# A long convolution with a routed expert on one core: placing products, gathers, fused scores, block loads and spectrum stores put elsewhere

## The chip, the cores and the metric

The kernel runs on one core of a Trainium2 chip. Its time is the device time of one execution in microseconds (us); the median of a few executions is given. The core has a matrix engine (TensorE, PE in the profile; PEld is its weight load), a vector engine (VectorE, DVE), a scalar engine (ScalarE, ACT), a general engine (GpSimd, POOL) and a queue engine (SyncE, SP) that here issues nearly all transfers. Each engine works through its own instructions in order, and waits for the others by semaphores. Transfers run on 16 DMA engines.

## The reference

Four sequences x and v of 12608 rows and 128 channels. A filter is made from position features, and applied along each sequence as a causal convolution (by FFT in the reference); the result is multiplied by x. Then a gate scores every row, the 128 best rows of each sequence go through a two-layer network, and its output, weighted by a sigmoid of the score, is added to those rows.

```python
h = (np.maximum(pos_emb @ w1, 0) @ w2) * np.exp(-0.01 * pos)[:, None]
y = irfft(rfft(x * v, 2*S, axis=1) * rfft(h, 2*S, axis=0)[None], 2*S, axis=1)[:, :S]
z = x * y                                      # [4, 12608, 128]
scores = z @ w_gate                            # per batch: the 128 largest, e
out = z;  out[e] += sigmoid(scores[e])[:, None] * (relu(z[e] @ w1m) @ w2m)
```

## The kernel before

**Shape of the work.** The convolution is done as a two-dimensional transform (93 by 125 points) with matrices held in SBUF. The work of one batch is 32 groups of four channels. After its 32 groups a batch has all its transformed outputs in one large SBUF tile, `big` (seen as `ay`, one slice of 2 x 126 x 4 numbers per group), and a column loop finishes it: 16 blocks of eight columns in the order `ORD`, in 32 half blocks h = 0 to 31 of four columns.

**The group step.** The main loop (L1140 to L1230) runs steps t = 0 to 130, over all four batches without a break. Step t holds, in program order: `turn(t - 3)`, the inverse products of the group three steps back (TensorE L515, copied out by ScalarE at L519 into `ay` and at L520 into a small tile); `dft`, the second forward product of group t (TensorE L313; ScalarE copies half of it at L316); hooks for background work; `f_s1(t + 1)`, the first forward product of the next group (TensorE L455, copied by ScalarE at L457); `load_u`, the loads of x and v four groups ahead (SP L292, 250 KB each, x into four buffers and v into two); `f_v`, `f_u` and `f_y`, eight VectorE operations (L464, L461, L471 four times, L473, L475) that combine group t and multiply group t - 1 by the filter's spectrum; on GpSimd `f_sd` (L482, L483, a recombination of group t - 1), `f_c` (L556, corrections of outputs) and `stage_u` (L298, the product x times v of three groups ahead); the loads of spectra (`load_h`, L302, two groups ahead, from the second batch on) and `put`, which moves a quarter of the outputs to other partitions (L532).

**Spectra.** The filter's spectra of the 32 groups are made once at the start, and lie in the upper part of `big` (`hh`, from element 8448 on, 744 elements each). Batch 0 reads them there. They are also stored to a DRAM tile `hd` (L1191, 372 KB each), from which the later batches load them, and batch 0's outputs are then written over them in `big`: group g covers elements 1008 g to 1008 g + 1007, and is written in steps g + 3 and g + 4. Before, step t stores the spectra 4(t-1)//3 up to 4t//3, so that all are stored after step 24.

**The column loop.** After the last group of a batch `P1.run` does for each half block h: `mm` (TensorE L601 and L605), `fin`: a VectorE product with the block of x (L616), and the scores. A score is either weighed and summed, by a product over four columns (L660, on VectorE, or on GpSimd for blocks past column 80) and four ScalarE sums (L670), or, in the last batch for h in `FU`, done by four VectorE products with a sum (L653). When a block is done it is stored to the output by SP (L644, 420 KB), and SP loads the block seven places later into the buffer of the one stored before (L578). Blocks of x for the first places of `ORD` are loaded ahead, during the groups, if their buffer is not one that the groups use: `AHEAD` is (0, 1, 2, 5, 6, 7), in half loads of 210 KB, one in each of the steps that `LA` names (batch 0: 12 in a row; later batches: every second group). The places 3 and 4 use buffers of the group loop and are loaded at the start of the column loop. `comb` (L588) prepares some columns on GpSimd. At h = 29 one `stage_u` is issued.

**Background work.** The top-128 selection of batch b runs during the groups of batch b + 1, as a generator `topk_one` that stops at points marked "e", "d", "n", "t", "p" and "w"; the main loop calls `bg.hook(kind, wait)` at fixed places of a step, and the generator goes on if it stands at that kind and at least `wait` steps have passed. At the end stands `place`: at "p" 16 matmuls (L308) multiply the ranks with a one-hot matrix that VectorE finishes at L944, then at "e" points five small VectorE steps (L954, L958, L964) make the row indices `ix`. At "w" `gather` (L973) lets GpSimd issue an indirect load of the chosen rows into `xe`. The chosen rows of the first three batches are used in the last column loop (h = 4, 8, 12 and 14); the fourth batch's selection stands alone at the end. Before each column loop, and at the first step after the last group (t = 128), `bg.drain` runs what is left.

**Order.** The order of all instructions on each engine is the program's order; semaphores are set where data overlap.

Of the kernel before, what the change touches and what calls it, by code (L numbers as in the profile page):

```python
# [23 lines left out]
NG = 32  # L24
# [14 lines left out]
NU, NV, NX, NH = 4, 2, 5, 3  # L39
# [4 lines left out]
Q4 = 4  # L44
NC, CO = 4, 2
NE = 2
LA = [range(32 - 14, 32 - 2)] + 3 * [range(6, 30, 2)]
NS, ND = 64, 4
SW = 50
NWARM = 8  # L50
# [3 lines left out]
CB = [k for k in ORD[2:] if k < JB]  # L54
NL, NM = 28, 7
DW = (4, 14)
FU = (7, 13, 19, 24, 28)
OFF, _o = {}, 0
for _n, _k, _w in (("te", 2, 2 * HW), ("qs", 2, HW), ("mt", 1, 2 * HW), ("yz", 2, 2 * HW), ("ws", 1, 2 * HW), ("sd", 2, 2 * HW),
                   ("ht", NH, 2 * HW), ("xa", NX, 8 * D), ("wx", 2, HB * D), ("cm", 2, 2 * NC * D), ("x", NU, XC), ("v", NV, XC)):  # L60
# [4 lines left out]
XE = [CE, OFF["yz"][0] + 2 * HW]  # L65
CE = [XE[0] + 8 * D, XE[1] + 8 * D]
XB = [OFF["xa"][0] + k * 8 * D for k in range(NX)] + XE
XB = [OFF["wx"][0]] + [XB[(i + NX - 2) % (NX + 2)] for i in range(len(ORD) - 1)]
AHEAD = [i for i in range(NX + 3) if XB[i] not in XE]
TE0, FS0, XC0 = 0, 4 * KC * FO, 4 * KC * FO + 2 * Q4 * 8 * FO  # L70
POS0, W0, HB0, WM0, CF0 = 0, PJ * NR, 8080, 8080 + N3 * FO, 8080 + N3 * (FO + 1)
HH0 = D * 2 * NJ - NG * 2 * HC
# [144 lines left out]
def hyena_moe(ctx, tc, xg, x2, pos, bw, ww, wg, mw1, mw2, cs, c1, gx, cf, ci, wm, tk, out):  # L217
# [18 lines left out]
    def buf(name, k, shape):  # L236
        o, n, w = OFF[name]
        return view(arena, o + k % n * w, shape)

    def small(shape, name, dt=F32, tag=None):  # L240
        return sp.tile(shape, dt, tag=tag, name=name, bufs=2 if tag == "sc" else 1)
# [8 lines left out]
    def ps2(k, shape, name):  # L250
        return view(bank2[k], 0, shape)

    def gap(n):
        return bank1[1][:, HC:HC + n]
# [39 lines left out]
    def stage_u(t):  # L294
        if t >= B * NG:
            return
        x, v = buf("x", t, [NP, XC]), buf("v", t, [NP, XC])
        nc.gpsimd.tensor_tensor(out=x, in0=x, in1=v, op=ALU.mult)  # L298
# [262 lines left out]
    class P1:  # L561
# [46 lines left out]
        def fin(self, h):  # L608
# [7 lines left out]
            nc.vector.tensor_tensor(out=xa[:, js], in0=self.s4.pop(h)[:, :n], in1=xa[:, js], op=ALU.mult)  # L616
            if self.last and h in FU:
                self.weigh()
# [56 lines left out]
        def run(self, ex):  # L675
            self.last = ex is not None
            self.ring = (0, 1, 2) if ex else (3, 2, 0, 1)
            self.wx = [OFF["wx"][0], OFF["wx"][0] + HB * D, OFF["te"][0] + (2 * HW if ex else 0),
                       OFF["sd"][0] if ex else OFF["ht"][0] + ((self.b + 1) * NG + 2) % NH * 2 * HW]
            self.wg = ps2(2, [128, D], f"wg_{self.b}")  # L680
            nc.scalar.copy(out=self.wg, in_=wgb)
            for i in range(NX + 3):
                if i not in AHEAD:
                    self.load_a(i)
            for k in range(2):
                self.comb()
            for h in range(len(self.hbs)):
                self.mm(h)
                self.fin(h)
                if h == 29:  # L690
                    stage_u((self.b + 1) * NG + 5)
                if ex:
                    ex.hook(h, self.wg)
            self.weigh()
            if ex:
                self.mask()
# [3 lines left out]
    class Background:  # L700
# [7 lines left out]
                self.kind = next(self.gen, None)  # L708
                self.at = self.now

        def drain(self):
            while self.kind is not None:
                self.hook(self.kind)

    def tots(rhs, lhs, n, nm, k):
# [256 lines left out]
    def gather(b, ix, xe):  # L972
        nc.gpsimd.indirect_dma_start(out=xe, out_offset=None, in_=of[:(b + 1) * PR * NJ],  # L973
                                     in_offset=bass.IndirectOffsetOnAxis(ap=ix, axis=0))
# [112 lines left out]
    def topk_one(b, p1, ex):  # L1087
        sc = p1.sc
        for a in range(0, len(p1.late), NM):
            yield "e"  # L1090
            p1.sums(p1.late[a:a + NM])
            yield "n"
        if p1.late:
            yield "d"
            m = gap(NJ)
            nc.scalar.copy(out=m, in_=negm)
            yield "e"
            p1.mask(m)
        f = small([128, NJ], f"f_{b}", tag="f")
        hi, *ms = (small([128, NJ], f"{t}_{b}", BF16, tag=t) for t in ("hi", "ms0", "ms1"))  # L1100
        k = (TopKS if b + 1 < B else TopK)(b, sc, onesb, f, hi, ms)
        k.ex = ex
        if ex:
            ex.start()
        yield from k.rounds()
        yield "n"
        if ex:
            xe = view(arena, OFF["yz"][0], [128, D])
            gather(b, ex.picked[0][1], xe)
        else:  # L1110
            xe = small([128, D], f"xe_{b}", tag=f"xe{b}")
        ws = buf("ws", 0, [128, 640])
        rk, oh = yield from select(b, k, NJ, tri, onesb, rst, ws)
        ix = yield from place(b, rk, oh, jio, NJ, 3, ws[:, :128])
        yield "w"
        gather(b, ix, xe)
        if ex:
            warm(NWARM)
            ex.one(b, ix, xe)
        else:  # L1120
            picked.append((b, ix, xe))
# [5 lines left out]
    bg = Background(iter(()))  # L1127
# [11 lines left out]
    for t in range(NT + LAG):  # L1139
        g = t % NG  # L1140
        i = t - LAG
        bg.now = t
        done = turn(i) if i >= 0 else []
        if t < NT:
            pq = [bank2[2 - 2 * (t % 2) + e] for e in range(2)]
            spare[0] = [a[:, 512 - NS:] for a in bank1]
            uv[t] = [a[:, :HC] for a in pq]
            qs = dft(t, te.pop(t), uv[t])
            if t == 0:
                rest()  # L1150
            bg.hook("p", 1)
            spare[0] = [pq[0][:, HC:]]
            bg.hook("t", 1)
            spare[0] = [a[:, 512 - NS:] for a in bank1]
            bg.hook("n", 1)
            for k in ((1, 2), (3,), (4,), (5,), ())[t] if t < 5 else (t + 1,):
                if k < NT:
                    te[k] = f_s1(k, ps=banks[6:] if k == 2 else bank1)
            spare[0] = None
            bg.hook("w", 1)  # L1160
            if t != 4:
                load_u(t + NU + (t < 4))
            if 0 <= t - 4 < len(fills):
                z = fills[t - 4]
                nc.scalar.activation(out=z, in_=one.to_broadcast([128, z.shape[1]]), func=AF.Copy, scale=0.0)
            o = t - 1 in uv
            if o:
                steps = f_y(t - 1, uv.pop(t - 1))
                y = next(steps)
                next(steps)  # L1170
            small_steps()
            f_v(uv[t], qs)
            if o:
                next(steps)
            bg.hook("e")
            f_u(uv[t], qs)
            seam = i >= 0 and i % NG == NG - 1
            now = [k for k in done if seam or k % NG == NG - 3]
            done_ = [k for k in done if k not in now]
            for k in now:  # L1180
                f_c(k)
            if o or t - 1 in ys:
                sd[t - 1] = f_sd(t - 1, y if o else ys.pop(t - 1))
            for k in done_:
                f_c(k, (ALU.subtract,))
            if not seam and t != 4:
                stage_u(t + 3 + (t < 4))
            for k in done_:
                f_c(k, (ALU.add,))
            for k in range(4 * (t - 1) // 3, min(4 * t // 3, NG)) if t else ():  # L1190
                nc.sync.dma_start(hd[:, k], hh[:, k].rearrange("p e s i -> p (e s i)"))  # L1191
            load_h(t + 2)
            for k in due + [k for k in done if k % NG >= NG - 3]:
                put(k, *((JM, NJ) if k % NG >= NG - 3 else ()))
            due = [k for k in done if k % NG < NG - 3]
            for _ in range(NE):
                bg.hook("e")
            if i >= 0 and i % NG == NG - 1:
                *_, ys[t] = f_y(t, uv.pop(t))
            if t == NT - 1:  # L1200
                sd[t] = f_last(t, uv.pop(t))
        if t >= NT:
            for k in due:
                put(k)
            due = []
            for k in done:
                f_c(k)
                put(k, *((JM, NJ) if k % NG >= NG - 3 else ()))
        if t == NT:
            bg.drain()  # L1210
            ex = Experts(picked)
        if t >= NT:
            for _ in range((3, 1, 0)[t - NT]):
                bg.hook("p")
                bg.hook("t")
                small_steps()
            bg.hook("w", 1)
        b = i // NG
        if i >= 0 and i % NG in LA[b]:
            if i % NG == LA[b][0]:  # L1220
                ph[b] = P1(b)
            k, e = divmod(LA[b].index(i % NG), 2)
            ph[b].load_a(AHEAD[k], e * HB, (e + 1) * HB)
        if i % NG == NG - 1 and i >= 0:
            bg.drain()
            p1 = ph.pop(b)
            p1.run(ex)
            bg = Background(topk_one(b, p1, ex))
    while bg.kind is not None:
        bg.hook(bg.kind)  # L1230
# [49 lines left out]
```

## Time and profile before

| | |
|---|---|
| time, median of 3 (lowest, highest) | 810.06 us (808.38, 812.73) |
| the profiled execution: its time, its span | 810.49 us, 808.6 us |
| granted TensorE clock, mean | 0.993 |
| busy: TensorE, VectorE, GpSimd, ScalarE | 96%, 86%, 76%, 71% |
| filter spectra made and first groups | to about 93 us |
| column loops | from about 231, 398, 568 and 726 us |
| selection of the last batch and its expert | from about 768 us |
| moved by DMA | 189.91 MB, mean 235 GB/s |

The profile is of one execution. Times are from the start of the span. A row of the timeline is one instruction or several equal ones in a row (x48), with its start, its length, engine, line, operation, what it writes and reads, and in brackets how long its engine stood idle before it and who ended that. Lengths of consecutive operations on one engine overlap somewhat, so a pace is read from starts. "issue" as the one waited for means that the profile shows nobody. SPq is a transfer's issue.

### The profile page before, as it was taken

The page shows a single profiled execution, that of the slowest core. Times are in us where ns is not written, and L with a number is a line of the kernel's source. Part 1 is how long each engine was busy: PE and PEld are TensorE (multiplying, and loading weights), DVE is VectorE, ACT ScalarE, POOL GpSimd, SP SyncE. Part 2 cuts the span into 40 slices and gives each one's busy share as a digit, 9 for nine tenths or more (in the row PEclk, how much of TensorE's full clock was granted, in tenths as well). Part 3 has the DMA queues.
Part 4 walks back from the last instruction along what each step waited for, and adds up shares of the span by engine and source line. Part 5 has one row for each costly group of instructions (what it writes and reads, how often), then busy time and mean ns, then how long its engine had stood idle before and what let it go on. Part 6 is the DMA issues. An engine that isn't in the chain of part 4 may idle for free. (4 is left out here: it accounts for less than half of the span.)

```text
span 808.6 us, 41568 instructions
## 1 busy us (share of the span) xinstructions
PE 775.7 (96%) x17154; PEld 651.5 (81%) x17154; DVE 698.7 (86%) x1713; ACT 576.4 (71%) x2269; POOL 618.1 (76%) x694
## 2 busy tenths in 40 slices
PE   8999999999999999999999998999999999989986
PEld 8999767987789678777898786877997787769865
DVE  7454699999879899999898999899999999988973
ACT  0345667665669889975699897866798988747751
POOL 1100189999979799998997998889987999987711
PEclk9999999999999999999999999999999999999998
DMA  9100279999978899998889899898898999847810
GB/s 323 64 27 3 85 238 294 308 307 269 254 240 268 288 263 279 292 293 242 244 274 311 258 286 258 251 280 253 255 301 268 283 287 282 266 124 236 280 48 14
DMA packets 82909, 189.91 MB, mean 235 GB/s; under 512 B 10552, under 2 KB 46264, under 8 KB 82720
## 3 DMA queue, kind: packets, MB, share of 16 engines
q1 hardware_dynamic: 82432, 186.67, 75.2%
q8 instruction: 135, 2.21, 1.2%
q0 software_dynamic: 288, 0.59, 0.3%
q14 instruction: 54, 0.44, 0.2%
HBM read 136.26 MB, written 39.55 MB: 217 GB/s over the span
## 5 line engine op out<-in xcount | busy, mean ns | idle before, releaser
L515 PE MATMUL b<-ci_sb,arena 128*31 128x126 f32 x6080 | 200.4, 271 | 7.8 <-issue 5.6
L455 PE MATMUL a<-c_sb,arena 128*32 128x186 f32 x4064 | 194.7, 321 | 4.0 <-issue 3.4
L298 POOL TENSOR_TENSOR arena<-arena 128x500 f32<-128x500 f32 x128 | 162.4, 1269 | 42.9 <-DMA arena<-in_xg_dram 42.8
L313 PE MATMUL c<-arena,cf_sb 128*32 128x372 f32 x2032 | 194.0, 477 | 0.9 <-DVE arena L473 0.6
L515 PEld LDWEIGHTS b<-ci_sb,arena 128*31 128x31 f32 x6080 | 177.9, 109 | 18.9 <-issue 8.9
L482 POOL TENSOR_TENSOR arena<-arena 128x372 f32<-128x372 f32 x127 | 116.2, 915 | 85.8 <-DVE arena L475 77.6
L457 ACT COPY arena<-a 128x372 f32<-128x372 f32 x252 | 119.9, 476 | 86.6 <-PE a L455 81.5
L455 PEld LDWEIGHTS a<-c_sb,arena 128*32 128x32 f32 x4064 | 139.4, 109 | 46.0 <-issue 20.0
L670 ACT ACTIVATE arena<-arena 128x128 f32<-128x128 f32 x479 | 140.7, 296 | 19.2 <-DVE arena L660 15.7
L519 ACT COPY big<-b 128x412 f32<-128x412 f32 x190 | 108.5, 573 | 19.0 <-PE b L515 17.2
L483 POOL TENSOR_TENSOR arena<-arena 128x372 f32<-128x372 f32 x127 | 115.8, 912 | 0.0
L313 PEld LDWEIGHTS c<-arena,cf_sb 128*32 128x32 f32 x2032 | 78.3, 109 | 44.1 <-issue 17.1
L556 POOL TENSOR_TENSOR big<-big,arena 128x184 f32<-128x184 f32 x192 | 112.5, 587 | 1.2
L471 DVE TENSOR_TENSOR c<-c,arena 128x372 f32<-128x372 f32 x190 | 103.3, 544 | 0.0
L471 DVE TENSOR_TENSOR arena<-c,arena 128x372 f32<-128x372 f32 x190 | 101.5, 534 | 0.0
L464 DVE TENSOR_TENSOR c<-c,arena 128x372 f32<-128x372 f32 x128 | 70.2, 549 | 23.1 <-ACT arena L316 17.7
L670 ACT ACTIVATION_READ_ACCUMULATOR arena<-arena 128x1 f32 x479 | 90.0, 188 | 0.0
L588 POOL TENSOR_TENSOR arena<-big 96x512 f32<-96x512 f32 x64 | 79.5, 1271 | 0.1
L461 DVE TENSOR_TENSOR c<-c,arena 128x372 f32<-128x372 f32 x128 | 70.1, 548 | 0.2
L316 ACT COPY arena<-c 128x372 f32<-128x372 f32 x128 | 61.2, 478 | 12.5 <-PE c L313 10.0
L473 DVE TENSOR_TENSOR arena<-c,arena 128x372 f32<-128x372 f32 x127 | 67.6, 533 | 0.0
L475 DVE TENSOR_TENSOR arena<-arena,c 128x372 f32<-128x372 f32 x127 | 67.4, 530 | 0.0
(216 smaller groups left out, 1262.8 us busy)
## 6 DMA issues: line engine op xcount, KB each, us to landing
arena<-in_xg_dram SPq DMA_DIRECT2D x256, 250.0 KB, 4.7
arena<-hd SPq DMA_DIRECT2D x96, 372.0 KB, 5.1
out_dram<-arena SPq DMA_DIRECT2D x60, 420.0 KB, 5.6
arena<-in_x_dram SPq DMA_DIRECT2D x36, 420.0 KB, 4.9
hd<-big SPq DMA_DIRECT2D x32, 372.0 KB, 5.0
big<-big SPq DMA_DIRECT2D x84, 126.0 KB, 5.2
arena<-in_x_dram SPq DMA_DIRECT2D x48, 210.0 KB, 5.2
big<-in_pos_dram SPq DMA_DIRECT2D x7, 496.0 KB, 7.5
```

The lines of the kernel that those rows point to most:

```text
L298: nc.gpsimd.tensor_tensor(out=x, in0=x, in1=v, op=ALU.mult)
L313: nc.tensor.matmul(pq[w][a:a + 32], lhsT=cf_sb[:, 2 * w + a // NQ, a % NQ:a % NQ + 32], rhs=te[:, a // NQ], start=True, stop=True)
L455: nc.tensor.matmul(tps[s // 2][c, s % 2], lhsT=u[:, s, c], rhs=c1_sb[:, k], start=True, stop=True)
L457: nc.scalar.copy(out=te[:, :, 2 * h:2 * h + 2].rearrange("p e s i -> p s e i"), in_=tps[h])
L471: nc.vector.tensor_tensor(out=o, in0=uv[e], in1=ht[:, k], op=ALU.mult)
L482: eng.tensor_tensor(out=nat(sd[:, 0]), in0=nat(yz[:, 0]), in1=rev(yz[:, 1]), op=ALU.add)
L483: eng.tensor_tensor(out=nat(sd[:, 1]), in0=rev(yz[:, 0]), in1=nat(yz[:, 1]), op=ALU.subtract)
L515: nc.tensor.matmul(o3[32 * k:32 * k + NT3, s % 2, e * NJ:(e + 1) * NJ], lhsT=d[:, e, s, c], rhs=ci_sb[:, e], start=True, stop=True)
L519: nc.scalar.copy(out=ay[:, t % NG, :NJ + JM, ss], in_=o3[:, :, :NJ + JM].rearrange("p s x -> p x s"))
L556: nc.gpsimd.tensor_tensor(out=d if op == ALU.subtract else a, in0=a, in1=stg(t), op=op)
L588: nc.gpsimd.tensor_tensor(out=cm[:KP, e].rearrange("p j (g s) -> p j g s", s=4), in0=av[0], in1=av[1], op=op)
L670: nc.scalar.activation(out=x, in_=x, func=AF.Copy, accum_out=self.sc[:, j:j + 1])
```

## The change

- `LA` and `AHEAD`: four places (0, 1, 2, 5) are loaded ahead in place of six, in eight half loads: in batch 0 in the last eight steps in which it was done before, in the later batches after every third group. Places 6 and 7 are loaded at the start of `P1.run`, behind places 3 and 4.
- `FU`: of the last batch's half blocks 13, 24 and 28 have fused scores; 7 and 19 are weighed and summed.
- The hook for "p" waits for two steps.
- The hook for "w" in the group step is gone. In the column loop one stands after h = 29, behind the `stage_u` there; the drain before the column loop stops at "w", and a full drain stands behind the loop. The third batch's gather is then run by the drain at t = 128.
- The spectra are stored one in each of the steps 1 to 32.

```diff
-LA = [range(32 - 14, 32 - 2)] + 3 * [range(6, 30, 2)]
+LA = [range(32 - 10, 32 - 2)] + 3 * [range(6, 30, 3)]
-FU = (7, 13, 19, 24, 28)
+FU = (13, 24, 28)
-AHEAD = [i for i in range(NX + 3) if XB[i] not in XE]
+AHEAD = [i for i in range(NX + 3) if XB[i] not in XE][:4]
...
                 if h == 29:
                     stage_u((self.b + 1) * NG + 5)
+                    bg.hook("w")
...
-        def drain(self):
-            while self.kind is not None:
+        def drain(self, upto=None):
+            while self.kind not in (None, upto):
                 self.hook(self.kind)
...
-            bg.hook("p", 1)
+            bg.hook("p", 2)
...
             spare[0] = None
-            bg.hook("w", 1)
...
-            for k in range(4 * (t - 1) // 3, min(4 * t // 3, NG)) if t else ():
+            for k in range(t - 1, t) if 0 < t <= NG else ():
                 nc.sync.dma_start(hd[:, k], hh[:, k].rearrange("p e s i -> p (e s i)"))
...
-            bg.drain()
+            bg.drain("w")
             p1 = ph.pop(b)
             p1.run(ex)
+            bg.drain()
```

## Rows read from the trace of the kernel before

**Rows 1.** Stages: stretch, length, each engine's busy us (instructions), clock, DMA share, GB/s.

```profile
189.00:231.00 42.00, 38.82 (x922) 31.08 (x916) 35.01 (x76) 24.20 (x59) 38.37 (x48) 1.00 0.92 249
399.00:410.00 11.00, 11.00 (x207) 11.00 (x204) 10.42 (x18) 9.38 (x63) 10.34 (x10) 1.00 0.78 222
```

**Rows 2.** Timeline, batch 0: inverse products and the first VectorE operation of two steps.

```profile
132.70 0.54 DVE L464 TENSOR_TENSOR c<-c,arena 128x372 f32<-128x372 f32 x1
133.16 1.48 PE L515 MATMUL b<-ci_sb,arena 128*31 128x126 f32 x48
136.31 0.54 DVE L464 TENSOR_TENSOR c<-c,arena 128x372 f32<-128x372 f32 x1
136.97 1.48 PE L515 MATMUL b<-ci_sb,arena 128*31 128x126 f32 x48
```

**Rows 3.** Timeline: the placing products in the second batch's groups, and VectorE beside them.

```profile
370.83 0.54 DVE L471 TENSOR_TENSOR arena<-c,arena 128x372 f32<-128x372 f32 x1
370.98 0.43 PE L308 MATMUL a<-arena 128*32 128x64 f32 x16 [0.18 <-DVE arena L944]
```

**Rows 4.** Timeline: the first gather, TensorE's waits behind it, the batch's last groups.

```profile
382.97 1.13 POOL L973 DMA_INDIRECT xe<-out_dram,ix  x1 [0.17 <-issue]
385.96 0.85 PE L515 MATMUL b<-ci_sb,arena 128*31 128x126 f32 x24 [0.44 <-POOL arena L483]
387.71 1.25 PEld L455 LDWEIGHTS a<-c_sb,arena 128*32 128x32 f32 x32 [0.32 <-POOL arena L298]
394.28 0.55 DVE L464 TENSOR_TENSOR c<-c,arena 128x372 f32<-128x372 f32 x1 [2.30 <-ACT arena L316]
```

**Rows 5.** Timeline: around the third gather, before the last group.

```profile
718.09 0.53 DVE L475 TENSOR_TENSOR arena<-arena,c 128x372 f32<-128x372 f32 x1
719.15 0.91 POOL L482 TENSOR_TENSOR arena<-arena 128x372 f32<-128x372 f32 x1
```

**Rows 6.** Timeline: GpSimd at the end of the second column loop.

```profile
431.71 1.26 POOL L298 TENSOR_TENSOR arena<-arena 128x500 f32<-128x500 f32 x1
434.09 1.28 POOL L660 TENSOR_TENSOR arena<-arena,wgb 128x512 f32<-128x512 f32 x1 [1.13 <-DMA out_dram<-arena]
```

**Rows 7.** Timeline: behind the fused scores of h = 19 in the last loop.

```profile
756.24 1.09 PE L605 MATMUL c<-big,gx_sb 96*64 96x128 f32 x16 [0.40 <-DVE arena L616]
757.63 0.31 ACT L670 ACTIVATE arena<-arena 128x128 f32<-128x128 f32 x1 [1.87 <-POOL arena L660]
```

**Rows 8.** Whom TensorE waited for, 269 to 726 us: total us, times, longest.

```profile
PE b L515 <- issue: 3.6, 5, 1.1
PE a L455 <- issue: 2.8, 3, 1.0
PE a L308 <- DVE arena L944: 0.5, 3, 0.2
```

**Rows 9.** Stages of 4 us, one in batch 0 and one in batch 3.

```profile
128.00:132.00 4.00, 4.00 (x104) 2.94 (x100) 4.00 (x10) 3.00 (x9) 4.00 (x6) 1.00 0.96 291
680.00:684.00 4.00, 3.11 (x84) 2.50 (x73) 3.33 (x10) 3.75 (x15) 4.00 (x6) 1.00 1.03 324
```

**Rows 10.** Timeline: one of TensorE's issue gaps.

```profile
684.11 1.15 PE L455 MATMUL a<-c_sb,arena 128*32 128x186 f32 x24 [1.01 <-issue]
```

**Rows 11.** Timeline: the spectrum load of step 30, the output copy of step 32.

```profile
209.05 1.22 SPq L302 DMA_DIRECT2D arena<-hd  x1
213.91 0.56 ACT L519 COPY big<-b 128x412 f32<-128x412 f32 x1 [0.34 <-PE b L515]
```

**Rows 12.** DMA issues, 186 to 222 us: count, KB each, median us to landing.

```profile
arena<-hd SPq DMA_DIRECT2D x4, 372.0 KB, 6.7
```

**Rows 13.** DMA issues of the whole span, the same columns.

```profile
hd<-big SPq DMA_DIRECT2D x32, 372.0 KB, 5.0
arena<-in_x_dram SPq DMA_DIRECT2D x48, 210.0 KB, 5.2
```

**Rows 14.** Timeline: VectorE's wait for a block, end of the second column loop.

```profile
431.39 0.69 DVE L616 TENSOR_TENSOR arena<-b,arena 128x512 f32<-128x512 f32 x1 [1.20 <-DMA arena<-in_x_dram]
```

## The prediction

> **What bounds the kernel now.** I read the stage windows first. In the last groups of the first batch TensorE, VectorE and GpSimd are busy for 38.8, 35.0 and 38.4 of 42 us, at the start of the second column loop for 11.0, 10.4 and 10.3 of 11, the DMA engines for 0.92 and 0.78 [rows 1]. So there is no one busy engine to relieve, and the question is which engine's wait ends last in each stage. Second, the timeline of two neighbouring group steps: TensorE starts the same block of inverse products every 3.81 us (133.16 to 136.97), while VectorE's step takes 3.61 us (132.70 to 136.31) [rows 2]. In plain groups TensorE sets the pace and VectorE follows 0.2 us faster; wherever a group carries selection work VectorE is the slower one. Third, the idle gaps of TensorE. From 269 to 726 us they sum to little, and the largest entry is "issue": 3.6 us in 5 gaps and 2.8 us in 3, together 6.4 us, of up to 1.1 us each, for which no engine answers [rows 8]. The rest are waits for GpSimd near the end of a batch [rows 4].
>
> The sums below are against the profiled execution's own 810.49 us (span 808.6 us). That execution lies 0.43 us above the median of 810.06, so 0.43 us is taken off at the end.
>
> **Placing products one group later.** Before, TensorE reaches them while VectorE still writes the second operand, and stands 0.18 us for it [rows 3], 0.5 us in the three batches [rows 8]. But the next VectorE operation starts at 370.83 without a gap: VectorE is the slower engine in these groups, and TensorE would have waited for it anyway. The 16 matmuls and the five small VectorE steps behind them are the same, a group later, still before the last groups of the batch. I take 0. Bounds: -0.5 us and +0.4 us (one run of the 16 matmuls, 0.43 us, meeting a group in which TensorE is last).
>
> **Gathers in the next column loop.** Removed from GpSimd's queue in the group loop: 1.13 us at 382.97 [rows 4], and two like it. GpSimd is in order and busy; behind the gather the two recombinations and the next u product run late, and TensorE stands 0.44 us for the one and 0.32 us for the other [rows 4]: 0.76 us. That alone costs nothing while VectorE is last, but it comes two groups before the end of the batch, where VectorE itself stands 2.30 us for what TensorE and ScalarE deliver (394.28) [rows 4]. So I count it whole, twice: 1.52 us. The third gather sits directly before the last group: its input is done at 718.09 + 0.53 = 718.62, the recombination starts at 719.15 [rows 5], 0.53 us. Together -2.05 us. What is added: the first two gathers now come after the u product at h = 29 of the column loop. There GpSimd ends at 431.71 + 1.26 = 432.97 and then stands 1.13 us until 434.09 [rows 6]; a gather of 1.0 to 1.13 us fits into that. Nothing waits for its data until the last column loop. If that cover is gone the recombination after it starts up to 1.1 us later. The third is issued in the drain of the first step after the last group, where it delays corrections of the last groups; I take 0. Bounds of all: -3.4 us (three times 1.13 all exposed) and +3.4 - 2.05 = +1.3 us.
>
> **Three fused scores.** At h = 7 and 19 of the last loop, four fused products with sum (DVE) become one weighing product (DVE) and four sums (ACT). After each fused block TensorE stands for VectorE, 0.40 us at 756.24 and about as long at h = 7 [rows 7]: -0.8 us. ScalarE gets four sums of 0.31 us each time, 1.2 us; it stands idle 1.87 us just there [rows 7], which covers them. Without the cover: +1.2 us each. Bounds -0.8 and +1.6 us.
>
> **Four column blocks ahead.** In each batch 12 half loads of 210 KB in the groups become 8 [rows 13], every third group in place of every second. Where the DMA engines' share is 0.96 (128 to 132 us) TensorE is busy for all 4.00 us; where it is 1.03 (680 to 684 us) it is busy 3.11 us, and there lies one of the issue gaps, 1.01 us [rows 9, 10]. So I read the gaps as instructions that arrive late when the transfers back up. The Trainium skill speaks against that reading: its page "DMA: Bandwidth & Descriptors", section "Queues, rings and completion order", says that each DMA engine goes round between its queues packet by packet, and "Runtime: NRT & Kernel Launch", section "Instruction fetch mechanics", that the fetch of the next block is mostly hidden. By those the load would not matter to the gaps, and this term would be 0. The rows show a gap where the share passes 1 and none at 0.96, so I follow the rows, in part: a third of the added load is gone, queues near full empty faster than in proportion, half of 6.4 us: -3.2 us. Bounds: 0 and -6.4 us.
>
> The two blocks (2 x 420 KB = 0.86 MB) are loaded at the start of each column loop instead. In its first 11 us the DMA engines are busy 0.78 at 222 GB/s [rows 1]: 2.4 us are free, room for 0.7 MB at 222/0.78 = 285 GB/s. The rest, 0.16 MB, is 0.6 us; SP's two added issues stand before the first store of the loop. The stores are waited for by later loads, so a third of this may last to the end of the loop, where VectorE already stands 1.20 us for a block [rows 14]: +0.2 us a loop, +0.8 us in four. Bounds: 0, and 0.86 MB at 285 GB/s = 3.0 us a loop, +12 us.
>
> **Spectra one a group.** Before, 32 stores of 372 KB [rows 13] are out after group 24; now eight of them (3.05 MB) fall into groups 25 to 32, into the stretch 189 to 231 us. There the DMA engines are busy 0.92 of 42 us at 249 GB/s [rows 1]: 3.4 us are free, 0.9 MB at 271 GB/s. 2.1 MB does not fit, 7.9 us of transfer. Second, a new wait: the outputs of group g are written over the spectra. Group 29's (written in step 32) lie over spectra 27 to 29, and spectrum 29 is now stored in step 30 instead of 23. That store would leave SP just before the load at 209.05; the copy that overwrites it starts at 213.91 [rows 11]. Transfers of this size take 6.7 us in this stretch [rows 12]: 209.05 + 6.7 - 213.91 = 1.8 us late. Behind that copy in ScalarE's queue is the copy of the next forward products, for which VectorE and then TensorE wait, so these 1.8 us count. Of the 7.9 us most is bridged (buffers a few groups deep, the thin first microseconds of the column loop); I take 1.7 us. Against it the lighter groups 1 to 24, which TensorE paces anyway, give 0. Sum +3.5 us. Bounds: -2.6 us (the stretch's three gaps at the group products vanish, as part of the issue idle before 231 us) and 1.8 + 7.9 = +9.7 us.
>
> **Sum.** -2.05 - 0.8 - 3.2 + 0.8 + 3.5 = -1.75 us; 810.49 - 1.75 - 0.43 = 808.3 us. Half a per cent, 4.05 us, is about what can be told from no change here: faster is below 806.0, slower above 814.1.
>
> **Rivals.**
> 1. Relief prevails: the issue gaps after the first batch go altogether (-6.4) and the late spectra cost nothing: -2.05 - 0.8 - 6.4 + 0.8 = -8.45, 801.6 us. For it: the gap that rows 9 and 10 date lies at a share above 1. Against: eight loads a batch remain.
> 2. The gaps do not depend on the transfers (term 0): +3.2, 811.5 us. The two pages named above say so. For it: 291 GB/s pass without a gap at 128 us [rows 9]. Against: the other row there.
> 3. The late spectra decide in full: ScalarE's copy of step 32 waits and the transfers behind it stay late into the column loop, +9.7 in place of 3.5: 814.5 us. It decides once the store of spectrum 29 takes more than the 4.9 us between 209.05 and 213.91, and passes half a per cent once the two together exceed 9.3 us.
> 4. The column loops turn to DMA: the two more loads push the first stores back, each later load waits for a store, and the last block comes 3.0 us later in each of four loops: +12 in place of 0.8, 819.5 us. For it: rows 14. Against: the free 22% at the start. It decides from 1.7 us a loop.
>
> **Chances.** My forecast 0.45, its own range 803.5 to 813; rival 1 0.27, rival 2 0.12, rival 3 0.09, rival 4 0.07. Faster: 0.26 of rival 1 and 0.05 of the forecast, 0.31. Slower: 0.05 of rival 3, 0.06 of rival 4, 0.03 of the forecast's and rival 2's tails, 0.14. The same: 0.55. The range 800.5 to 815 leaves out about 0.1 below and 0.08 above.
>
> **What would show it.** TensorE's waits for GpSimd two groups before each column loop gone, and no new idle of GpSimd after h = 29. Issue idle of TensorE after 269 us near 3 us. In the steps 32 to 34 a ScalarE copy that waits for the store of spectra, 1 to 4 us. At the column loops' ends VectorE's wait for a block no longer than 1.5 us. In the last loop two of TensorE's waits after fused blocks gone. I am wrong if the first batch loses over 6 us or nothing, if the gaps stay at 6 us, or if a column loop grows by over 1 us.

## The result, and the profile after

Over 20 executions each, the changed kernel took 816.22 us (median; 809.79 to 822.96), the kernel before 810.07 us (802.89 to 819.35). The medians lie 6.15 us apart. The ratio used from here on compares all executions except those in a slow state, and is 1.0061, 95% interval 1.0039 to 1.0084: slower by 3.2 to 6.8 us. The forecast of 808.3 us was on the wrong side, and 816.2 lies above its range. The traced execution of the changed kernel (809.79 us, span 808.0) is the fastest of its twenty, so the two first traces do not differ by what the kernels differ by; stages are compared over several traces below.

VectorE's waits for transfers, changed kernel, whole span (total us, times, longest):

```profile
DVE arena L616 <- DMA arena<-in_x_dram: 10.6, 11, 1.7
DVE arena L660 <- DMA out_dram<-arena: 2.3, 2, 1.7
```

Before, the first of these was 2.1 us in 2 waits, 1.20 of it in [rows 14]. The second column loop as it ends, VectorE's waits for blocks of x:

```profile
426.12 0.69 DVE L616 TENSOR_TENSOR arena<-b,arena 128x512 f32<-128x512 f32 x1 [1.18 <-DMA arena<-in_x_dram]
432.10 0.69 DVE L616 TENSOR_TENSOR arena<-b,arena 128x512 f32<-128x512 f32 x1 [1.59 <-DMA arena<-in_x_dram]
434.65 0.69 DVE L616 TENSOR_TENSOR arena<-a,arena 128x512 f32<-128x512 f32 x1 [0.66 <-DMA arena<-in_x_dram]
```

Three waits stand where one stood. From the last group operation ahead of the loop to the first behind it:

```profile
393.36 0.55 DVE L464 TENSOR_TENSOR c<-c,arena 128x372 f32<-128x372 f32 x1 [1.36 <-ACT arena L316]
...
436.71 0.55 DVE L464 TENSOR_TENSOR c<-c,arena 128x372 f32<-128x372 f32 x1
```

This distance, 43.35 us, is called the length of the loop here; before it ran from 394.28 [rows 4] to 435.33, 41.05 us. In the first row the wait ahead of the operation is 1.36 us where it was 2.30 us: that is the gather and the placing products, which moved together. The same two stages as [rows 1]:

```profile
189.00:231.00 42.00, 39.75 (x948) 31.30 (x941) 35.69 (x77) 23.75 (x63) 39.67 (x48) 1.00 1.00 304
399.00:410.00 11.00, 11.00 (x206) 10.98 (x204) 9.92 (x17) 10.04 (x67) 9.08 (x8) 1.00 0.84 269
```

The end of the first batch has gone from 249 to 304 GB/s and a share of 1.00. The first 11 us of the column loop carry 269 GB/s, not 222, so the free time there was used in part, and the loop became longer all the same.

ScalarE's output copies in the steps 31 to 33, which wait for the stores of the spectra that they overwrite, and the transfers between 186 and 222 us (count, KB each, median us to landing):

```profile
211.55 0.56 ACT L519 COPY big<-b 128x412 f32<-128x412 f32 x1 [2.29 <-DMA hd<-big]
216.76 0.56 ACT L519 COPY big<-b 128x412 f32<-128x412 f32 x1 [1.25 <-DMA hd<-big]
221.87 0.55 ACT L519 COPY big<-b 128x412 f32<-128x412 f32 x1 [0.90 <-DMA hd<-big]
```

```profile
hd<-big SPq DMA_DIRECT2D x8, 372.0 KB, 5.9
```

The copy waited 0.34 us, for TensorE, in [rows 11]; now 4.4 us in three copies. TensorE's waits on "issue" between 269 and 726 us, against the 6.4 us of [rows 8]:

```profile
PE b L515 <- issue: 1.3, 3, 0.6
PE a L455 <- issue: 0.7, 2, 0.5
PE c L308 <- issue: 0.5, 1, 0.5
PE c L313 <- issue: 0.3, 1, 0.3
```

2.8 us. And the moved gather on GpSimd, behind h = 29 of the second loop [rows 6]:

```profile
432.02 1.25 POOL L298 TENSOR_TENSOR arena<-arena 128x500 f32<-128x500 f32 x1
433.44 1.12 POOL L974 DMA_INDIRECT xe<-out_dram,ix  x1 [0.16 <-issue]
435.48 1.28 POOL L660 TENSOR_TENSOR arena<-arena,wgb 128x512 f32<-128x512 f32 x1 [0.92 <-DVE arena L616]
```

After the gather GpSimd still waits 0.92 us for VectorE: the gather is hidden, as forecast. TensorE's matmul behind h = 19, which had waited 0.40 us [rows 7], starts without a wait:

```profile
755.41 1.04 PE L605 MATMUL c<-big,gx_sb 96*64 96x128 f32 x16
```

### The profile page after: what moved, and what is told of

Its sections match the earlier page's. It is cut to its first block, busy times and chain, and to the rows that moved or that the text cites. A ratio compares the mean times of both kernels' runs of the same rounds, so it can differ in the third digit from the quotient of the medians.

```text
span 808.0 us, 41564 instructions
## 1 busy us (share of the span) xinstructions
PE 776.5 (96%) x17154; PEld 648.5 (80%) x17154; DVE 696.5 (86%) x1699; ACT 580.1 (72%) x2285; POOL 617.7 (76%) x694
## 5 line engine op out<-in xcount | busy, mean ns | idle before, releaser
L482 POOL TENSOR_TENSOR arena<-arena 128x372 f32<-128x372 f32 x127 | 117.9, 928 | 80.8 <-DVE arena L475 73.6
L455 PEld LDWEIGHTS a<-c_sb,arena 128*32 128x32 f32 x4064 | 136.9, 110 | 49.8 <-issue 19.0
L670 ACT ACTIVATE arena<-arena 128x128 f32<-128x128 f32 x487 | 143.7, 306 | 18.1 <-DVE arena L660 17.9
L483 POOL TENSOR_TENSOR arena<-arena 128x372 f32<-128x372 f32 x127 | 117.8, 927 | 0.0
L556 POOL TENSOR_TENSOR big<-big,arena 128x184 f32<-128x184 f32 x192 | 115.0, 600 | 1.2
L313 PEld LDWEIGHTS c<-arena,cf_sb 128*32 128x32 f32 x2032 | 74.5, 109 | 49.7 <-issue 20.2
L471 DVE TENSOR_TENSOR c<-c,arena 128x372 f32<-128x372 f32 x190 | 104.9, 552 | 0.0
L471 DVE TENSOR_TENSOR arena<-c,arena 128x372 f32<-128x372 f32 x190 | 103.3, 544 | 0.0
L670 ACT ACTIVATION_READ_ACCUMULATOR arena<-arena 128x1 f32 x487 | 96.3, 198 | 0.0
L464 DVE TENSOR_TENSOR c<-c,arena 128x372 f32<-128x372 f32 x128 | 71.3, 557 | 19.4 <-ACT arena L316 17.6
L316 ACT COPY arena<-c 128x372 f32<-128x372 f32 x128 | 61.4, 480 | 16.3 <-PE c L313 10.1
L461 DVE TENSOR_TENSOR c<-c,arena 128x372 f32<-128x372 f32 x128 | 71.3, 557 | 0.2
L473 DVE TENSOR_TENSOR arena<-c,arena 128x372 f32<-128x372 f32 x127 | 69.6, 548 | 0.0
```

The source lines that it names most:

```text
L313: nc.tensor.matmul(pq[w][a:a + 32], lhsT=cf_sb[:, 2 * w + a // NQ, a % NQ:a % NQ + 32], rhs=te[:, a // NQ], start=True, stop=True)
L455: nc.tensor.matmul(tps[s // 2][c, s % 2], lhsT=u[:, s, c], rhs=c1_sb[:, k], start=True, stop=True)
L471: nc.vector.tensor_tensor(out=o, in0=uv[e], in1=ht[:, k], op=ALU.mult)
L482: eng.tensor_tensor(out=nat(sd[:, 0]), in0=nat(yz[:, 0]), in1=rev(yz[:, 1]), op=ALU.add)
L483: eng.tensor_tensor(out=nat(sd[:, 1]), in0=rev(yz[:, 0]), in1=nat(yz[:, 1]), op=ALU.subtract)
L556: nc.gpsimd.tensor_tensor(out=d if op == ALU.subtract else a, in0=a, in1=stg(t), op=op)
```

## The experiments

A ratio is against executions of the kernel before on the same chip; one ahead, one column and before, again, were executed once. Lengths in us, read from the starts of VectorE's first operation of a step (L464); "27-33" is from step 27 to step 34, the loops are as defined above, the last one from its first to its last product with x (L616). "Issue" is TensorE's wait of that name from 269 to 726 us. The last two columns are of steps 27 to 33 alone: how long ScalarE's output copies waited there for stores of spectra, and TensorE's wait on "issue".

| kernel | ratio to before (95%) | 27-33 | loop 1 | loop 2 | loop 3 | last | issue | 27-33: copies | 27-33: issue |
|---|---|---|---|---|---|---|---|---|---|
| before | | 32.7 | 42.4 | 41.1 | 40.6 | 39.9 | 6.4 | 0 | 2.6 |
| before, again | | 29.4 | 42.5 | 40.5 | 42.3 | 39.9 | 10.1 | 0 | 0.2 |
| changed | 1.0061 (1.0039 to 1.0084) | 32.2 | 43.8 | 43.4 | 43.6 | 39.1 | 2.8 | 4.8 | 1.7 |
| changed, again | 1.0056 (1.0016 to 1.0097) | 32.2 | 44.4 | 43.5 | 44.5 | 42.2 | 6.1 | 4.2 | 1.9 |
| six ahead | 0.9973 (0.9937 to 1.0009) | 32.2 | 44.6 | 41.1 | 40.6 | 38.7 | 6.8 | 0.4 | 2.7 |
| old spectra | 0.9997 (0.9963 to 1.0031) | 28.9 | 44.2 | 43.8 | 44.5 | 40.5 | 3.6 | 0 | 0 |
| both back | 0.9953 (0.9921 to 0.9985) | 31.9 | 41.7 | 41.6 | 40.8 | 38.7 | 6.6 | 0 | 2.2 |
| one ahead | once: 827.09 us | 31.5 | 49.4 | 48.5 | 47.8 | 44.0 | 4.1 | 0 | 1.7 |
| loads behind stores | 0.9982 (0.9948 to 1.0015) | 32.9 | 43.6 | 42.2 | 42.0 | 38.8 | 4.1 | 4.5 | 2.2 |
| spread | 0.9961 (0.9929 to 0.9992) | 29.5 | 41.4 | 40.5 | 41.0 | 38.7 | 11.8 | 0 | 0.4 |
| late loads | 1.0023 (0.9988 to 1.0058) | 31.2 | 42.2 | 41.6 | 40.7 | 38.7 | 15.3 | 0 | 0.2 |
| loads behind stores, old spectra | 0.9956 (0.9926 to 0.9987) | 28.9 | 43.4 | 42.0 | 42.2 | 38.7 | 2.7 | 0 | 0 |
| one column | once: 801.85 us | 32.2 | 40.8 | 40.6 | 40.9 | 38.7 | 4.1 | 1.5 | 1.9 |

**Both kernels once more**, unaltered.

> The changed kernel once more, unaltered, for a second trace. The first trace is of its fastest execution (809.79 us; median 816.22), so something varies between executions. Theory A (column loops and late spectra are the fixed cost, the issue gaps of TensorE are what varies): the four column loops last as in the first trace within 0.5 us each, the ScalarE copies wait for stores of spectra 3 to 5 us in steps 31 to 33 again, and the issue gaps after 93 us come to another sum than 5.5 us, near the 10.8 us of the kernel before. Theory B (the column loops vary): issue gaps near 5.5 us again, and a loop over 1 us longer or shorter. Time 1.003 to 1.009 of before.

> The kernel before, once more, for a second trace of it. Theory A (stages repeat, issue gaps vary): column loops within 0.7 us of 42.4, 41.1 and 40.6; steps 61 to 65 and 93 to 97 at 21.2 and 20.7 us; issue gaps in the groups of batches 1 to 3 again 5 to 8 us. Theory B (what I put down to the gathers and the loads is spread between executions): one of these stages differs by over 1 us.

Loops 1 to 3 of the changed kernel sum to 130.8 and 132.4 us in its two traces, those of before to 124.1 and 125.3. The distance of 6 to 7 us stays, though loops vary more than theory A of the first run allowed: those of one kernel differ by up to 1.7 us, and the changed kernel's last loop by 3. Its copies waited again in steps 31 to 33, 3.8 us in two copies and not in three. Its waits for blocks in the second trace:

```profile
DVE arena L616 <- DMA arena<-in_x_dram: 15.5, 19, 1.7
```

Issue gaps do vary, as theory A said (2.8 and 6.1 us; 6.4 and 10.1). The second trace of before:

```profile
PE b L515 <- issue: 6.9, 9, 1.2
PE c L313 <- issue: 1.9, 2, 1.2
PE a L455 <- issue: 1.3, 1, 1.3
```

Steps 61 to 65 lasted 21.2 us in both traces of before, 20.7 and 19.7 us in those of the changed kernel; steps 93 to 97 20.7 and 22.3 us, then 19.7 and 19.8. Here and in loop 3 the second trace of before is 1.6 to 1.7 us off the first, more than theory A allowed; theory B's condition is met. So a difference of under 1.7 us between two single traces proves little by itself; the terms below are means over several traces where there are several.

**Six blocks ahead again.**

```diff
-LA = [range(32 - 10, 32 - 2)] + 3 * [range(6, 30, 3)]
-AHEAD = [...][:4]
+LA = [range(32 - 14, 32 - 2)] + 3 * [range(6, 30, 2)]
+AHEAD = [...]
```

> The changed kernel with six column blocks ahead again, in twelve half loads per batch as before; the rest of the change stays. Theory A (the two extra block loads at the start of each column loop put the stores and so the later loads back): VectorE's waits for blocks of x fall from 10.6 us to under 4, the intervals over the first three column loops return to within 0.5 us of 42.4, 41.1, 40.6, and the time is 5 to 8 us below the changed kernel, about 0.993 of it, at or below before. Theory B (the loops are long because of the late spectra or the gather behind h = 29): loops stay at 43.4 to 43.8, time unchanged. If the half loads cause issue gaps, as I forecast, the gaps grow by 3 to 6 us and eat half of the gain.

0.9973/1.0061 = 0.991 of the changed kernel, 7 us. VectorE waits for no block at all in any loop; loops 2 and 3 are back at 41.1 and 40.6. Loop 1 is not (44.6), but not through blocks: it lost 2.5 us at its start, where TensorE stood 2.0 us on issue. The gaps from 269 us came back too:

```profile
PE b L515 <- issue: 6.3, 5, 2.2
PE a L455 <- issue: 0.5, 1, 0.5
```

**The spectra as before.**

```diff
-            for k in range(t - 1, t) if 0 < t <= NG else ():
+            for k in range(4 * (t - 1) // 3, min(4 * t // 3, NG)) if t else ():
```

> The changed kernel with the spectra stored four in three groups as before; the rest stays. Theory A (each late store makes the ScalarE copy that overwrites a spectrum wait): the waits for stores of spectra in steps 31 to 33 (4.4 us) vanish, the steps 27 to 33 shrink by 2 to 3 us, the column loops do not change; time 0.996 to 0.998 of the changed kernel. Theory B (the transfers of the late spectra make the first column loop late): the first loop alone also shrinks by over 1 us.

0.9997/1.0061 = 0.9936, 5 us; against the changed kernel's second run, on the same chip, the intervals overlap, so the size rests on the trace: steps 27 to 33 shrink from 32.2 to 28.9 us, no copy waits for a store there, and TensorE has no issue gap there. The column loops do not shrink, and theory B falls. Theory A's waits came out, and the steps shrank even by a little more than its 2 to 3 us, but the last two columns of the table speak against its reason: the copies' waits do not order the lengths, as the account below says. The end of the first batch, first in the changed kernel, then with the old stores (stretch, length, busy TensorE, its weight loads, VectorE, ScalarE, GpSimd, clock, DMA share, GB/s):

```profile
204.00:216.00 12.00, 11.34 (x287) 8.38 (x281) 10.52 (x24) 6.80 (x17) 11.83 (x16) 1.00 1.03 325
216.00:228.00 12.00, 10.41 (x238) 8.33 (x229) 7.64 (x17) 6.60 (x16) 9.84 (x13) 1.00 1.04 304
```

```profile
204.00:216.00 12.00, 12.00 (x312) 11.36 (x307) 11.40 (x26) 8.69 (x21) 12.00 (x15) 1.00 0.91 259
216.00:228.00 12.00, 12.00 (x269) 10.56 (x263) 9.90 (x21) 6.42 (x21) 11.76 (x15) 1.00 0.91 275
```

At a share of 0.91 TensorE is busy throughout; at 1.03 it stands for 2.2 of 24 us.

**Both put back**: the two diffs together.

> The changed kernel with both the six blocks ahead and the old stores of spectra: only the gathers, the placing products and the fused scores are changed against before. Theory A: the sum of the two experiments before, 2 to 4 us below before (0.995 to 0.998). Theory B (gathers and fused scores gain nothing, the gain is only that of the gaps): 0.999 to 1.001 of before.

0.9953 of before, 3.8 us faster (1.2 to 6.4): the gathers, the placing and the fused scores alone are a gain, theory A. No run sets them apart from one another.

**One block ahead.**

```diff
-LA = [range(32 - 10, 32 - 2)] + 3 * [range(6, 30, 3)]
-AHEAD = [...][:4]
+LA = [range(32 - 4, 32 - 2)] + 3 * [(6, 18)]
+AHEAD = [...][:1]
```

> The changed kernel with one block ahead (two half loads per batch) in place of four; the blocks of the other places are loaded at the start of the column loop. It sorts two questions. Issue gaps in the groups of the batches 1 to 3 (269 to 726 us before): with twelve half loads 6.2, 6.8 and 6.4 us in three traces, with eight 2.5, 5.9 and 3.7. Theory A (gaps come with the transfers): under 2.5 us with two. Theory B (independent, the difference was luck): 4 to 7 us. Column loops: theory A (each byte that a loop moves more costs its transfer time, 420 KB at 285 GB/s = 1.5 us a block): the second and third loop last 41 + 5 x 1.5 = 48 to 49 us. Theory B (the two loads cost by their place ahead of the first stores, and the stores wait anyway): under 46 us.

Loops 2 and 3 last 48.5 and 47.8 us, 7.1 us (mean) more than the mean of 41.0 us with six ahead: 1.4 us for each of five blocks, close to the transfer time of 420 KB, as theory A had it. Issue gaps from 269 us:

```profile
PE b L515 <- issue: 3.4, 6, 1.1
PE c L313 <- issue: 0.5, 1, 0.5
PE a L455 <- issue: 0.2, 1, 0.2
```

4.1 us, at the lower edge of theory B's numbers and far over theory A's. But B's reason, luck, does not fit the other traces: the five with twelve evenly spaced half loads have 6.4 to 11.8 us, the six with eight 2.7 to 6.1. So some 4 us come whatever is loaded ahead, and the rest comes with the loads; their number and their spacing changed together.

In loops 2 and 3 of this kernel VectorE waited 3.6 and 0.6 us for blocks of x, and 3.6 and 3.7 us for a store that still had to read the buffer which a weighing product overwrites:

```profile
416.54 0.69 DVE L660 TENSOR_TENSOR arena<-arena,c 128x512 f32<-128x512 f32 x1 [3.57 <-DMA out_dram<-arena]
```

**The two loads behind the first stores.**

```diff
-                if i not in AHEAD:
+                if i not in AHEAD and i < 6:
...
                 if i > 1:
                     self.load_a(i - 1 + NX + len(XE))
+                else:
+                    self.load_a(i + 6)
```

> The changed kernel with the loads of places 6 and 7 issued behind the stores of the first two blocks of a column loop, not ahead of them: the same bytes in another order on SP. Theory A (the loop as a whole moves too many bytes): VectorE still waits for blocks by 6 us or more in all and the second and third loop stay within 1 us of 43.4 to 44.5 us. Theory B (order: the loads hold up the first stores, and the loads behind these in SP's queue): the loop's first later load issues at 12 to 13 us and not at 15 to 16 us after the last group, and the loops return to under 42 us; time 0.994 of the changed kernel.

**One column of those two blocks.**

```diff
-                    self.load_a(i)
+                    self.load_a(i, 0, 8 if i < 6 else 1)
```

> The changed kernel with one column of eight loaded for places 6 and 7 at the start of a column loop (52 KB in place of 420 KB each, the same number of issues in the same place); the rest of these two blocks stays what the buffer held. Theory A (bytes): VectorE's waits for blocks fall from 10.6 to 15.5 us to under 4, the second and third loop return to 41 to 41.7 us. Theory B (two more issues ahead of the first stores on SP, whatever their size): they stay over 43 us.

SP's issues at the start of the second loop, in the changed kernel, with the loads behind the stores, and with one column:

```profile
397.14 2.97 SPq L578 DMA_DIRECT2D arena<-in_x_dram  x4
400.21 4.08 SPq L644 DMA_DIRECT2D out_dram<-arena  x3
408.80 0.34 SPq L578 DMA_DIRECT2D arena<-in_x_dram  x1
```

```profile
396.21 2.33 SPq L578 DMA_DIRECT2D arena<-in_x_dram  x2
398.63 0.36 SPq L644 DMA_DIRECT2D out_dram<-arena  x1
399.03 0.72 SPq L578 DMA_DIRECT2D arena<-in_x_dram  x1
400.65 0.93 SPq L644 DMA_DIRECT2D out_dram<-arena  x1
401.63 0.56 SPq L578 DMA_DIRECT2D arena<-in_x_dram  x1
403.04 0.95 SPq L644 DMA_DIRECT2D out_dram<-arena  x1
406.71 0.33 SPq L578 DMA_DIRECT2D arena<-in_x_dram  x1
```

```profile
395.59 2.80 SPq L578 DMA_DIRECT2D arena<-in_x_dram  x4
398.48 4.27 SPq L644 DMA_DIRECT2D out_dram<-arena  x3
404.78 0.34 SPq L578 DMA_DIRECT2D arena<-in_x_dram  x1
```

The last row of each is the first load that has to wait for a store, and everything later on SP stands behind it. From the starts of the loops (393.36, 392.44, 391.81) it goes out after 15.4, 14.3 and 13.0 us; before, after 13.3. With one column the number of issues and their place are those of the changed kernel, and loops 2 and 3 last 40.6 and 40.9 us: it is the bytes, not the issues. (The rest of those blocks keeps what the buffer held, so this kernel's output is wrong; its instructions are the same.) With the two loads behind the first two stores they last 42.2 and 42.0: the order gives back 1.4 and 2.2 us of the 2.5 and 3.2 that the loops had grown. So neither theory of order and bytes holds alone. By the ratios this order is worth 0.9982/1.0061 = 0.992.

**Two versions meant to beat both.** Six ahead, the first batch's half loads spread, the spectra eight in seven groups:

```diff
+LA = 4 * [range(6, 30, 2)]
+AHEAD = [...]
+            for k in range(8 * (t - 1) // 7, min(8 * t // 7, NG)) if t else ():
```

> A version meant to beat both: six blocks ahead, gathers, placing and fused scores as changed; in the first batch the twelve half loads in every second group from group 6 on, as in the other batches, and the spectra stored eight in seven groups, so that the last is out in step 28. Theory A (gaps at the end of the first batch come from the transfers there, and the late spectra's wait from too short a time before they are overwritten): steps 27 to 33 last 29 to 30 us as with old spectra and four ahead (28.9) and not 32, no wait for a store of spectra, the loops 41 to 42 us; time 0.990 to 0.994 of before. Theory B (the load only moves the gaps to earlier groups): groups 0 to 26 grow by 2 to 4 us over 100.0 and the time is that of the version with both put back, 0.995.

In this kernel some half loads of the first batch land before those buffers are filled with zeros, so part of that batch's output is made from zeros; instructions and transfers are those of the diff. Steps 27 to 33 fell to 29.5 us, as theory A had it, and the steps 0 to 26 grew to 102.0, from 99.9 and 100.2 in the changed kernel and 100.6 and 101.3 before. 0.9961 is no better than both put back: theory B for the time. Then six ahead with eight of the half loads in the selection's groups:

```diff
+LA = [range(32 - 14, 32 - 2)] + 3 * [(8, 12, 16, 20, *range(22, 30))]
+AHEAD = [...]
```

> A version meant to beat both: gathers, placing and fused scores as changed, spectra as before, six blocks ahead, but in the batches 1 to 3 eight of the twelve half loads in the groups 22 to 29, where the selection makes VectorE the slower engine (steps of 4.1 to 4.6 us) and the DMA engines' share is 0.70 to 0.96. Theory A (issue gaps come where the share passes 1): issue gaps of batches 1 to 3 fall from 6 to 10 us (twelve half loads in every second group) to 3 to 5 us, the column loops stay at 42, 41 and 41 us, time 0.990 to 0.994 of before. Theory B (only the number of half loads counts): gaps of 6 to 10 us as before, time 0.995; the end of the batch may wait for x and v.

Both theories missed. The end of the third batch, and the gaps from 269 us:

```profile
538.00:544.00 6.00, 5.36 (x135) 4.10 (x128) 6.00 (x14) 2.43 (x6) 4.77 (x6) 1.00 1.04 257
544.00:550.00 6.00, 4.51 (x113) 3.76 (x109) 4.97 (x15) 2.68 (x7) 5.25 (x7) 1.00 1.05 299
550.00:556.00 6.00, 4.73 (x123) 3.94 (x115) 4.71 (x12) 3.16 (x7) 4.87 (x6) 1.00 1.03 263
556.00:562.00 6.00, 4.76 (x127) 4.38 (x126) 3.73 (x10) 3.32 (x9) 4.09 (x6) 1.00 1.04 261
```

```profile
PE b L515 <- issue: 10.5, 12, 2.5
PE c L313 <- issue: 2.5, 3, 1.5
PE a L455 <- issue: 2.3, 4, 1.5
```

The share that I had meant to fill stays at 1.03 to 1.05 for 24 us, gaps rise to 15.3 us, and steps 93 to 97 take 27.3 us in place of 19.7. The same half loads, packed closer, nearly double the gaps: that they depend on the transfers is seen here most plainly, in one trace. VectorE waited for no block, the loops stayed, and the time was lost in the groups.

**The order of loads and the old spectra together.**

> Four blocks ahead, places 6 and 7 loaded behind the stores of the loop's first two blocks, spectra stored four in three groups as before; the rest as changed. Theory A (the parts add): steps 27 to 33 near 29 us in place of 32.9, no wait for stores of spectra, loops 42 to 43.6 us as with the other order alone, issue gaps of batches 1 to 3 near 4 us; time 0.992 to 0.995 of before. Theory B (the first column loop takes back what the batch's end gains): first loop 44 us or more and time 0.997 to 1.000.

```profile
PE b L515 <- issue: 2.4, 5, 0.9
PE c L308 <- issue: 0.3, 1, 0.3
```

0.9956 of before, 3.6 us faster (1.1 to 6.0). It reaches the same as both put back by another way: 28.9 us at the end of the first batch and 2.7 us of gaps, against loops that are still 3 us longer in sum. These two versions beat the kernel before and the changed one; between them nothing can be told.

## Why the prediction was wrong

**The step that failed** is the column loops' term: "a third of this may last to the end of the loop ...: +0.2 us a loop, +0.8 us in four". Measured, as the mean of the three traces with four loads at the loop's start and the old order (changed, again, old spectra) against the six with six ahead: 44.1 - 42.5, 43.6 - 41.1 and 44.2 - 41.0, +7.4 us in three loops, and in the last loop 40.6 against 38.7 (the four with six ahead and the new scores), +1.9: +9.2 us. The sign named in advance, a loop longer by over 1 us, came in all three (1.4, 2.3 and 3.0 us between the first traces). Two turns of the argument were wrong. I counted the 22% of free DMA time at the loop's start as room. Part of it was used (269 GB/s against 222), but the loads stand ahead of the first stores, and the first later load, which waits on SP for a store, went out 2 us later in the second loop. And I let two thirds of a delay decay; it did not: that loop as a whole became 2.3 us longer. With full blocks the loops are long and with one column of them they are not, so the bytes do it, and one ahead shows that each further block costs 1.4 us. The traces show the path: each later load waits for a store, and VectorE for the load, or for a store that must first read what VectorE overwrites. That was rival 4, priced at 3.0 us a loop and given 0.07; its price was about right (1.6, 2.5, 3.2 and 1.9). The block that comes 1.20 us late already [rows 14] was the row to weigh higher: here the chain of transfers already ended last, and the bytes added to it cost their time.

**Spectra, +3.5 us.** With four ahead in both, steps 27 to 33 last 32.2 us in two traces with the late stores and 28.9 in two without: +3.3. The size was right, but half of the mechanism is not borne out. The wait that I had named is there, in three copies and not in one: 2.29, 1.25 and 0.90 us against my 1.8. But it does not set the length. In six traces with late stores and the steps at 31.5 to 32.9 us the copies waited 0 to 4.8 us; before, no copy waited for a store, and the steps took 32.7 us all the same. What goes with the length is TensorE's wait on "issue": none in the two traces at 28.9 us, 0.2 and 0.4 us in those at 29.4 and 29.5, and 1.7 to 2.7 us in the eight from 31.5 to 32.9 (late loads, at 31.2, had 0.2 us of it and one wait of 1.2 us for GpSimd). So of my two items the second, the overload, is the one that the traces bear out: share 1.03 to 1.04 and 2.2 us of standing, against 0.91 and none. That the sum of the two came out near 3.3 is in part luck. The term also hangs on what else is loaded: with six ahead the late stores made steps 27 to 33 only 0.3 us longer (32.2 against 31.9 for both put back). Against before, whose own steps 27 to 33 took 32.7 and 29.4 us, the net is +1.1, because the four fewer half loads give something back there.

**Issue gaps, -3.2 us.** Mean of the five traces with twelve evenly spaced half loads 8.3 us, of the six with eight 3.9: -4.4. A third fewer loads took away about half of the gaps, as I had guessed without a row for it. The gaps cost time: the groups of batches 1 to 3, from the first step behind a loop to the last ahead of the next, lasted together 362.5 us (mean of the six with eight) against 367.2 (mean of the three evenly spaced with twelve and the gathers moved), -4.7. Rival 2, by which the gaps would not depend on the transfers, falls with the late loads. The Trainium skill's page "Runtime: NRT & Kernel Launch", section "Instruction fetch mechanics", lets one expect a fetch that is mostly hidden. If these gaps are late instructions, this kernel does not agree, with up to 15.3 us of them; that they are was argued from their name and is not shown. How the DMA engines take turns between queues no run here resolves.

**Gathers, -2.05 us, and placing, 0.** Steps 61 to 65 lost 1.0 us (21.2 to the mean of 20.7 and 19.7), steps 93 to 97 1.0 (20.7 to 19.7), the third gather's steps 0.1 (7.95 to 7.83): -2.1. The sum is right, in part by luck: the first two gave 1.0 and not 0.76 each, the third 0.1 and not 0.53, as step 125 lost 0.6 and step 126, where the placing steps now fall, gained 0.5. The second trace of before, with 22.3 us in steps 93 to 97 and an issue gap of 0.9 us among them, is left out of this.

**Fused scores, -0.8 us.** The last loop lasted 39.92 us in both traces of before and 38.74 in the four with six ahead: -1.2.

**The sum with the measured terms**: -2.1 - 1.2 - 4.4 + 9.2 + 1.1 = +2.6 us, somewhat below the measured 3.2 to 6.8. Stage by stage, without the terms, the means of the two traces of each kernel differ by +6.9 us in loops 1 to 3, +0.7 in the last loop, -5.5 in the groups of batches 1 to 3, +1.1 in steps 27 to 33, -0.9 in steps 0 to 26 and +1.4 elsewhere: +3.7 us. Part of the last is behind the last loop: from its last product with x to GpSimd's last instruction the second trace of the changed kernel and that with old spectra took 39.6 and 40.9 us, all others 37.6 to 38.4, the first trace of the changed kernel (38.2) and one ahead (38.4) among them. I had not seen it, and its cause is open.

## What to carry to other kernels

A transfer taken out of a busy stage is not free where it lands. In this loop, whose loads wait for stores and whose vector engine waits for both, each block of 420 KB added ahead of the first stores cost 1.2 to 1.6 us in loops 2 and 3, although the DMA engines showed 22% idle time at the loop's start. That this idle time is the chain's own waiting is argued and not shown; before counting such time as room, ask which transfer waits for which. A wait that a change adds is not yet its cost: here copies waited up to 4.8 us or not at all, in stages of the same length. And filling the stretch that looks emptiest can back the transfers up there: packing half loads closer took the gain away in the one run that tried it.

## What the runs showed of the hardware

The first matmuls behind the last column loop wait on "issue" for 0.98 us in ten traces of thirteen, that with one block ahead among them. In the other three the last loop had itself waited for blocks in its last 4 us; with one ahead it had waited for a block only earlier, 2.2 us at 745 us, 39 us before its last product. The changed kernel and the one with old spectra:

```profile
767.00 1.98 PE L308 MATMUL a<-arena 128*64 128x128 f32 x32 [1.29 <-issue]
```

```profile
766.88 3.47 PE L308 MATMUL a<-arena 128*64 128x128 f32 x30 [2.08 <-issue]
```

In the second trace of the changed kernel it is 2.97 us. So in these three traces, where a loop ended on late transfers, even matmuls that wait for no data in the profile came later. No experiment was made on this, and what those gaps are in the chip no run here settles.
